# A planned attention and gated-MLP kernel: q and k of four heads transposed in one piece, and a list scheduler with other ranks and another model of TensorE

## The chip, the cores and the metric

The kernel runs on one core of a Trainium2 chip. The metric is the device time in microseconds (us) from start to end of one execution; lower is better. The engines of the core are named as in the profile: PE (TensorE, matmuls), PEld (its weight loads), DVE (VectorE), ACT (ScalarE), POOL (GpSimd) and SP (SyncE, which here only issues DMAs). Each works through its own list of instructions in order. ACT issues some DMAs as well, and such an issue stands in ACT's list.

## The reference

```python
def _attn_ref(q, k, v, g_q, g_k):            # q, k, v: [8, 12, 448, 64] float32
    q_n, k_n = (rmsnorm(q, g_q), rmsnorm(k, g_k))
    scores = (1.0 / np.sqrt(64)) * np.matmul(q_n, k_n.transpose(0, 1, 3, 2))
    scores = scores - np.max(scores, axis=-1, keepdims=True)
    attn = np.exp(scores)
    attn = attn / (np.sum(attn, axis=-1, keepdims=True) + 1e-09)
    return np.matmul(attn, v)

def _moe_ref(x, mu_k, mu_r, w_k, w_v, w_r):  # x: [8, 448, 768]; w_k [768, 1024], w_v [1024, 768], w_r [768, 768], float64
    x_prev = x shifted by one row, zeros ahead
    xk = mu_k * x + (1.0 - mu_k) * x_prev
    xr = mu_r * x + (1.0 - mu_r) * x_prev
    k = np.maximum(xk @ w_k, 0.0)
    v = k * k @ w_v
    r = 1.0 / (1.0 + np.exp(-(xr @ w_r)))
    return r * v
```

The attention's output, with its 12 heads side by side, is the `x` of the second part.

## The kernel before

**Numbers as two halves.** Each float32 matrix that PE multiplies is split into a float16 high part and a float16 low part, and a product is three products of such parts (high x high, high x low, low x high). So most data appear twice, and each split is an ACT cast (high) and a DVE or POOL subtraction (low).

**Attention, in quads and groups.** A quad is four heads (two pairs) of one batch; there are 24 quads and 48 pairs. A quad goes through these steps:

- `load`: k and q of the quad from HBM into tiles `qk` (or, early, into space lent by `xk`). The 448 rows of a head are dealt as 64 rows of 7 blocks, so that one partition holds 7 x 64 contiguous numbers, and two heads of a pair fill 64 partitions.
- `stats`: ACT squares, POOL and DVE add them up, DVE takes a reciprocal root by three Newton steps on small tiles (`sst`, `stm`, `ss`).
- `preps`: POOL multiplies by the root, ACT casts to the high part, POOL subtracts for the low part (both in a tile `nat`), and SP issues DMA transposes from `nat` to `stk`, one of 64 rows for each pair and tensor: four for a quad.
- `scores`: 168 groups, seven for a quad. A group is 128 query rows of both heads of a pair against all 448 keys (6 matmuls, two PSUM banks `sc` of five); the fourth group of a quad takes the seventh block of both pairs (12 smaller matmuls).
- `expo`, `probs`, `split`: for each of the two banks DVE takes the row maximum, ACT the exponential with its row sum, DVE turns the sum into a factor (`sums`), ACT writes the high part of the probabilities and DVE the low part (`nat`), which frees the bank. SP then transposes `nat` to `pT` (128 rows; the fourth group in two pieces of 64 rows).
- `vload`, `vprep`: v of a pair is loaded in four DMAs (`vf`), scaled and split (`vh`, `vl`).
- `attends`: 24 matmuls per pair give `ot`, which ACT copies to `x`.

**The second part, per batch.** `mix` makes `xk` and `xr` from six `x` tiles (POOL, DVE, ACT, POOL for each). `moe` then runs 144 matmuls of `xk` with `wk`, squares the result (`kf`, `kk`), and runs blocks of 18 matmuls `xr` with `wr` and 24 matmuls `kk` with `wv` for each half: three blocks for an even batch, four for an odd one. `gate` and `store` finish a block and SP stores it. There is one `xk`, one `xr` and one `kk` buffer.

**The weights** come as float64 and are turned to float32, scaled and split in 20 column tiles (`wload`, `weights`, `wsplit`): 8 of `w_k`, 6 of `w_r`, 6 of `w_v`. For tiles in `POOL_TILES` POOL scales and subtracts, for the others DVE does. The first MoE product needs the first 8 tiles and batch 0's `xk`; the first `wr` block needs all 20.

**What sets the order.** All of this is written as generators, which `Plan.run` advances as a list scheduler. Each generator offers its next instruction; the planner keeps a clock for each engine from its own price list (`price`, and the costs in `emit`), finds by `ready` when the tiles' earlier readers and writers are done, and takes the instruction with the smallest `max(clock of the engine, ready time) - 0.1 * priority`. The order in which it emits is the order in each engine's list on the chip. The priorities are the constants `PRIO_*`; `MARGIN` holds attention matmuls back until they are surely ready. In `ready`, an instruction on PE that writes the bank that the matmul before it wrote is taken to wait for that one's end and some latency.

**Rings.** Tiles come from rings with a fixed number of buffers (`QK_BUFS`, `STK_BUFS`, `NAT_BUFS` and so on).

Of the kernel before, what the change touches and what calls it, by code (L numbers as in the profile page):

```python
# [15 lines left out]
P = 128  # L16
# [12 lines left out]
QK_BUFS = 4  # L29
# [3 lines left out]
STK_BUFS = 3  # L33
# [4 lines left out]
POOL_TILES = range(2, 20, 2)  # L38
# [6 lines left out]
PRIO_P = 400  # L45
PRIO_S = 250
PRIO_A = 100
# [5 lines left out]
XK_LENT = ("nat", "nat", "qk")  # L53
PRIO_K = 100
# [3 lines left out]
PRIO_M = 400  # L58
PRIO_W = 100
W_START = 10e3  # L60
W_GAP = 9e3
W_PUSH = 0.03
F64_EXP = 2.0 ** -112
# [16 lines left out]
class Op:  # L80
    def __init__(self, eng, fn, kw, form=None):
        self.eng, self.fn, self.kw, self.form = eng, fn, kw, form
        outs = [kw[k] for k in ("out", "accum_out") if kw.get(k) is not None]
        self.reads = [span(x) for k, x in kw.items() if k not in ("out", "accum_out") and hasattr(x, "tensor")]
        self.writes = [span(x) for x in outs if hasattr(x, "tensor")]
        self.reads = [x for x in self.reads if x]
        self.writes = [x for x in self.writes if x]
# [6 lines left out]
def span(x):  # L94
    t = x.tensor
    if "DRAM" in str(t.space):
        return None
    st = x.ap[0][0]
    lo = x.offset % st if st else 0
    return t.name, lo, lo + 1 + sum(abs(s) * (n - 1) for s, n in x.ap[1:])  # L100
# [48 lines left out]
class Plan:  # L149
# [16 lines left out]
    def ready(self, ops):  # L166
        r = 0.0
        for op in ops:
            for t, lo, hi in op.reads:
                for a, b, fin, wr in self.use.get(t, ()):  # L170
                    if wr and a < hi and lo < b and fin > r:
                        r = fin
            for t, lo, hi in op.writes:
                for a, b, fin, wr in self.use.get(t, ()):
                    if a < hi and lo < b and fin > r:
                        r = fin
# [13 lines left out]
    def note(self, op, fin):  # L190
        for spans, wr in ((op.reads, False), (op.writes, True)):
            for t, lo, hi in spans:
# [4 lines left out]
                u.append((lo, hi, fin, wr))  # L197

    def emit(self, ops):
# [7 lines left out]
        if e == "PE":  # L207
            form, cost = ops[0].form
            if form != self.form:
# [6 lines left out]
        elif ops[0].fn.__name__.startswith("dma"):  # L216
# [49 lines left out]
class Ring:  # L266
# [15 lines left out]
    def get(self, early=False):  # L282
# [13 lines left out]
        if old:  # L296
            self.plan.use[name] = [(0, 1 << 30, old, True)]
        return t

    def put(self, t):  # L300
# [5 lines left out]
        self.plan.use["slot " + tag] = max(x[2] for x in self.plan.use.pop(name))  # L306
# [3 lines left out]
def rsqrt(V, y, a, t):  # L310
# [3 lines left out]
    for _ in range(NEWTON):  # L314
        yield V.tensor_tensor(out=t, in0=a, in1=y, op=ALU.mult)
        yield V.scalar_tensor_tensor(out=t, in0=t, scalar=-0.5, in1=y, op0=ALU.mult, op1=ALU.mult)
        yield V.scalar_tensor_tensor(out=y, in0=t, scalar=1.5, in1=y, op0=ALU.add, op1=ALU.mult)


def attn_moe_kernel(tc, q, k, v, g_q, g_k, mu_k, mu_r, w_k, w_v, w_r, out):  # L320
# [19 lines left out]
    mu = const.tile([P, 2, ND], F32, name="mu")  # L340
    omu = const.tile([P, 2, ND], F32, name="omu")
# [18 lines left out]
    st = {"wdone": 0, "g": 0, "moe": 0, "vl": 0, "gm": False, "mus": False, "kdone": 0}  # L360
# [11 lines left out]
    def late():  # L372
# [8 lines left out]
        "stk": Ring(ap_, [P, 2, 2 * NT, HD], F16, "stk", STK_BUFS, plan),  # L381
        "pT": Ring(ap_, [P, 2 * NT, S], F16, "pT", PT_BUFS, plan),
# [11 lines left out]
    }  # L394
    HOME = {}
# [44 lines left out]
    def mu_stats():  # L440
        yield A.dma_start(out=mu[:, 0, :], in_=mu_k.rearrange("(t p) -> p t", p=P))
        yield A.dma_start(out=mu[:, 1, :], in_=mu_r.rearrange("(t p) -> p t", p=P))
        yield V.tensor_scalar(out=omu, in0=mu, scalar1=-1.0, scalar2=1.0, op0=ALU.mult, op1=ALU.add)
# [3 lines left out]
        yield V.tensor_scalar(out=u, in0=mu, scalar1=2.0, scalar2=-1.0, op0=ALU.mult, op1=ALU.add)  # L447
# [13 lines left out]
    def load():  # L461
        for u in range(NQ):
            b, j = quads[u]
            ts = []
            for n, src in enumerate((k, q)):
                t = yield from R["qk"].get(u < 3)
                for x in range(2):
                    h0 = 4 * j + 2 * x
                    yield (A if u < 2 else SP).dma_start(out=t[x * HD:(x + 1) * HD], in_=src[b, h0:h0 + 2].rearrange("h (r t) d -> r h (t d)", t=NT))
                ts.append(t)  # L470
            LD[u] = ts

    def stats():
        for u in range(NQ):
            yield from until(lambda: u in LD and st["gm"])
# [3 lines left out]
            for n, t in enumerate(LD[u]):  # L479
# [7 lines left out]
                if n == 0:  # L487
                    yield G_.tensor_tensor(out=tv, in0=tv, in1=bcast(G[:, :], 2 * NT), op=ALU.mult)
            yield V.tensor_scalar(out=ss[:, 0:2 * NT], in0=ss[:, 0:2 * NT], scalar1=1.0 / HD, scalar2=1e-6, op0=ALU.mult, op1=ALU.add)
            yield V.tensor_scalar(out=ss[:, 2 * NT:NSS], in0=ss[:, 2 * NT:NSS], scalar1=gm[:, 3:4], scalar2=gm[:, 4:5], op0=ALU.mult, op1=ALU.add)  # L490
            yield from rsqrt(V, y, ss, tm)
            SS[u] = y

    def preps():
        for u in range(NQ):
            yield from until(lambda: u in SS)
            y = SS.pop(u)
            X = []
            for x in range(2):
                t = yield from R["stk"].get(u < 3)  # L500
                X.append(t)
            for n, t in enumerate(LD.pop(u)):
                tv = t.rearrange("p h (t d) -> p (h t) d", d=HD)
                yield G_.tensor_tensor(out=tv, in0=tv, in1=spread(y[:, 2 * NT * n:2 * NT * (n + 1)], HD), op=ALU.mult)
                nat = yield from R["nat"].get(u < 3)
                hi, lo = heads(nat, 0), heads(nat, NT * P)
                t4 = t.rearrange("p h (t d) -> p h t d", d=HD)
                yield A.copy(out=hi, in_=t4)
                yield G_.tensor_tensor(out=lo, in0=t4, in1=hi, op=ALU.subtract)
                R["qk"].put(t)  # L510
                for x in range(2):
                    yield SP.dma_start_transpose(out=X[x][:, n], in_=nat[x * HD:(x + 1) * HD].rearrange("p a c -> p (a c)"))
                R["nat"].put(nat)
            for x in range(2):
                TQ[2 * u + x] = X[x]
# [45 lines left out]
    def batch_scales(b):  # L561
# [14 lines left out]
    def scores():  # L576
        for gi, (u, x, t0) in enumerate(groups):
            yield from until(lambda: 2 * u + x in TQ and len(banks["sc"].free) > 1)
# [6 lines left out]
            for m, (kl, ql) in enumerate(((0, 0), (0, 1), (1, 0))):  # L585
                for i in (2 * u + 1, 2 * u) if both_pairs else (2 * u + x,):
                    X = TQ[i]
                    for h in (1, 0):
# [10 lines left out]
            if t0 == NT - 1:  # L599
                R["stk"].put(TQ.pop(2 * u))  # L600
            elif x and t0 == NT - 3:
                R["stk"].put(TQ.pop(2 * u + 1))
            sums = ring_sum[gi % 6]
            D = {}
            for j in range(2):
                plan.spawn(expo(gi, j, both[j], sums, D), PRIO_E)
            plan.spawn(probs(gi, both, sums, D), PRIO_E)

    def expo(gi, j, sp, sums, D):
        yield V.tensor_reduce(out=sums[:, j:j + 1], in_=sp[:, 0:S], axis=AX.X, op=ALU.max, negate=True)  # L610
        yield A.activation(out=sp[:, 0:S], in_=sp[:, 0:S], func=AF.Exp, bias=sums[:, j:j + 1], accum_out=sp[:, S:S + 1])
        D[j] = True

    def probs(gi, both, sums, D):
        u, x, t0 = groups[gi]
        yield from until(lambda: len(D) == 2 and st["g"] == gi)
        for i in (2 * u, 2 * u + 1) if t0 == NT - 1 else (2 * u + x,):
            if i not in PT:
                PT[i] = yield from R["pT"].get()
# [5 lines left out]
        for j, sp in enumerate(both):  # L625
            yield V.tensor_scalar(out=r[:, j:j + 1], in0=sp[:, S:S + 1], scalar1=1e-9, scalar2=2.0 ** -15, op0=ALU.add, op1=ALU.mult)
# [6 lines left out]
        if t0 < NT - 1:  # L633
            yield SP.dma_start_transpose(out=PT[2 * u + x][:, :, t0 * HD:(t0 + 2) * HD], in_=phf)
            CNT[2 * u + x] += 1
        else:
            for y in range(2):
                yield SP.dma_start_transpose(out=PT[2 * u + y][:, :, t0 * HD:], in_=phf[y * HD:(y + 1) * HD])
                CNT[2 * u + y] += 1
# [286 lines left out]
```

## Time and profile before

| | before |
|---|---|
| median of 3 runs | 1139.08 us (1138.01 to 1139.62) |
| the profiled execution | 1136.72 us |
| its span, first to last instruction | 1134.6 us |
| mean granted TensorE clock | 0.952 |
| busy: PE, DVE, ACT, POOL | 917.6, 846.7, 757.7, 664.2 us |
| DMA packets, data moved | 480,163, 161.76 MB |
| first score matmul, first MoE matmul | 56.6, 197.7 us |
| last attend matmul ends | about 1003.4 us |

A row of the profile names the line of the kernel, the engine, the operation and the tiles (output, arrow, inputs). Every instruction is recorded at one line of the planner's `emit`, so the rows are told apart by their tiles. In a row of a group, `| busy, mean ns of one | idle time of the engine just before them` follow the count. DMA issues and semaphore waits are not counted as busy, so SP has no share of its own; its queue is read from rows with `SPq`, which give the shortest, median and longest duration of an issue. Matmuls are pipelined, so busy time of PE is more than the time that its columns need.

### The profile page before, as it was taken

The numbers are of one execution on the slowest core, as the hardware profiler recorded it, in microseconds if no ns is written. First come the engines' busy times: TensorE is split into PE (matmuls) and PEld (weight loads), VectorE is DVE, ScalarE is ACT, GpSimd is POOL, SyncE is SP. The second block draws the span as 40 slices with busy tenths as digits, with TensorE's granted clock in tenths as the row PEclk, the third lists the DMA queues.
The fourth block names the chain that finished last, engine by engine and source line by source line (L and its number), as shares of the span: only waits on it lengthen the run. The fifth ranks groups of instructions, "written<-read, shape, count | busy, mean of one in ns | idle before, by whom it ended". The sixth has DMA issues, their size and how long they took to land. (4 is left out here: it accounts for less than half of the span.)

```text
span 1134.6 us, 18939 instructions
## 1 busy us (share of the span) xinstructions
PE 917.6 (81%) x6031; PEld 474.5 (42%) x6031; DVE 846.7 (75%) x2254; ACT 757.7 (67%) x1750; POOL 664.2 (59%) x668
## 2 busy tenths in 40 slices
PE   1346445968989889898889898989898899999997
PEld 0112222424444444444444454444444444455564
DVE  5898797997899589879888987889786879822000
ACT  3577475896779577777778776788577768832310
POOL 2733328785678465685668574877486636463611
PEclk9996665989999999999999999999999999999999
DMA  9999999876988888897998888889886989811011
GB/s 194 196 182 181 168 188 208 156 142 129 170 168 143 160 146 165 154 156 146 147 167 150 155 161 158 156 141 171 148 141 125 171 135 159 140 26 28 14 29 28
DMA packets 480163, 161.76 MB, mean 143 GB/s; under 512 B 447296, under 2 KB 476480, under 8 KB 480064
## 3 DMA queue, kind: packets, MB, share of 16 engines
q1 hardware_dynamic: 459808, 141.42, 71.1%
q10 hardware_dynamic: 20256, 19.15, 6.8%
q8 instruction: 47, 0.77, 0.3%
q14 instruction: 52, 0.43, 0.1%
HBM read 50.40 MB, written 11.01 MB: 54 GB/s over the span
## 5 line engine op out<-in xcount | busy, mean ns | idle before, releaser
L205 ACT ACTIVATE sc<-sc,sums 128x448 f32<-128x448 f32 x336 | 201.1, 620 | 70.9 <-DVE sums L205 68.0
L205 PE MATMUL mm<-wvh,kk 128*128 128x384 f16 x896 | 236.3, 328 | 5.6 <-DVE o L205 4.7
L205 DVE SCALAR_TENSOR_TENSOR nat<-sc,sums,nat 128x448 f16<-128x448 f32 x316 | 201.2, 673 | 27.1 <-ACT nat L205 26.5
L205 PE MATMUL mm<-xk,wkh 128*128 128x448 f16 x768 | 209.9, 355 | 6.5 <-ACT kf L205 4.2
L205 DVE TENSOR_REDUCE sums<-sc 128x1 f32<-128x448 f32 x336 | 194.0, 611 | 18.5 <-PE sc L205 18.4
L205 ACT ACTIVATE nat<-sc,sums 128x448 f16<-128x448 f32 x316 | 187.7, 662 | 24.6 <-DVE sums L205 7.3
L205 PE MATMUL sc<-stk 64*128 64x448 f16 (+1 forms) x1152 | 133.8, 382 | 78.0 <-DVE nat L205 52.3
L205 PE MATMUL mm<-wrh,xr 128*128 128x384 f16 x672 | 177.3, 328 | 0.0
L205 PEld LDWEIGHTS <-kk 128*128 128x128 f16 (+1 forms) x1362 | 129.6, 99 | 110.9 <-issue 28.5
L205 PE MATMUL ot<-pT,vh 128*64 128x448 f16 x768 | 123.2, 376 | 39.6 <-DMA pT<-nat 20.2
L205 PE MATMUL mm<-wvl,kk 128*128 128x384 f16 x448 | 147.0, 328 | 0.0
L205 PE MATMUL mm<-xk,wkl 128*128 128x448 f16 x384 | 136.0, 354 | 0.0
L205 PEld LDWEIGHTS <-xr 128*128 128x128 f16 x1008 | 96.3, 98 | 73.8 <-issue 12.0
L205 POOL TENSOR_TENSOR nat<-qk,nat 128x896 f16<-128x896 f32 x45 | 87.7, 1948 | 65.9 <-ACT nat L205 65.7
L205 DVE SCALAR_TENSOR_TENSOR df<-x,bsc,df 128x448 f32<-128x448 f32 x96 | 99.8, 1050 | 29.2 <-POOL df L205 28.8
L205 POOL TENSOR_TENSOR o<-o,bsc 128x384 f32<-128x384 f32 x48 | 43.7, 910 | 117.2 <-DVE o L205 83.2
L205 PE MATMUL mm<-wrl,xr 128*128 128x384 f16 x336 | 109.9, 327 | 0.0
L205 PEld LDWEIGHTS <-stk 64*128 64x128 f16 (+1 forms) x1152 | 45.6, 101 | 150.4 <-issue 100.1
L205 PEld LDWEIGHTS <-wkh 128*128 128x128 f16 x768 | 70.8, 98 | 88.7 <-issue 31.9
L205 DVE SCALAR_TENSOR_TENSOR o<-o,mm 128x384 f32<-128x384 f32 x56 | 30.5, 544 | 94.6 <-PE mm L205 67.3
L205 POOL TENSOR_TENSOR kf<-kf 128x448 f32<-128x448 f32 x64 | 62.6, 979 | 56.1 <-ACT kk L205 54.1
L205 ACT ACTIVATE o<-mm,bsc 128x128 f32<-128x128 f32 x144 | 43.3, 386 | 70.1 <-PE mm L205 52.0
(129 smaller groups left out, 1625.0 us busy)
## 6 DMA issues: line engine op xcount, KB each, us to landing
out_dram<-o SPq DMA_DIRECT2D x56, 192.0 KB, 3.1
qk<-in_k_dram SPq DMA_DIRECT2D x44, 224.0 KB, 3.8
qk<-in_q_dram SPq DMA_DIRECT2D x42, 224.0 KB, 3.8
vf<-in_v_dram SPq DMA_DIRECT2D x96, 64.0 KB, 3.1
raw<-in_moe_w_v_dram ACTq DMA_DIRECT2D x12, 512.0 KB, 5.0
vf<-in_v_dram SPq DMA_DIRECT2D x96, 48.0 KB, 2.8
raw<-in_moe_w_r_dram ACTq DMA_DIRECT2D x12, 384.0 KB, 5.8
kk<-in_moe_w_k_dram ACTq DMA_DIRECT2D x8, 384.0 KB, 6.9
```

Source lines behind the costliest of these rows:

```text
L205: r = op.fn(op.kw["out"], op.kw["value"]) if op.fn.__name__ == "memset" else op.fn(**op.kw)
```

## The change

In the kernel's work:

- `stk` holds a quad instead of a pair: one transpose of 128 rows each for k and q. Two such tiles instead of three of half the size; three `qk` tiles instead of four.
- So that the blocks of q come out side by side, q is loaded in eight DMAs per quad (runs of 64 numbers) instead of two (runs of 448).
- `pT` of both pairs of a quad is one tile of two halves, and the seventh block's probabilities go there in one transpose of 128 rows. The odd pair's blocks stand in another order, and its copy from `ot` to `x` is done in two parts.
- The two row sums of a group are written side by side in the first bank, and one DVE instruction works on both. The scales of `mix` and of the output are made in fewer instructions.
- Quad 0's multiplies and subtractions go to DVE (`Q_DVE`), 13 weight tiles instead of 9 to POOL, and the weight loads wait until the first group is past its exponential (`W_G0`). The first pieces of k and q are loaded ahead of v and the weights.

In the scheduler: `span` tells the two halves of partitions and of `pT` apart; `ready` no longer lets a PE instruction wait for an earlier one on PE; priorities are other numbers, and some rise while `moe` waits for something (`st["want"]`, `BOOST_*`) or while few groups are left before a quad's data are needed (`near`, `SLACK_*`). `NEWTON_ON` stays on DVE and the three `*_SLOW` factors are 1.

The diff, cut to what the steps of the prediction touch:

```diff
-QK_BUFS = 4
+QK_BUFS = 3
-STK_BUFS = 3
+STK_BUFS = 2
-POOL_TILES = range(2, 20, 2)
+POOL_TILES = range(1, 14)
-PRIO_P = 400
+PRIO_P = 200
-PRIO_A = 100
+PRIO_A = 50
-XK_LENT = ("nat", "nat", "qk")
-PRIO_K = 100
+XK_LENT = ("qk", "qk", "nat")
+PRIO_K = 0
+BOOST_K = 500
+BOOST_R = 500
+BOOST_A = 300
+BOOST_W = 300
+BOOST_Q = 400
+SLACK_S = 3
+SLACK_Q = 2
+W_G0 = 1
+LOAD_A = 2
+Q_DVE = 1
...
                 for a, b, fin, wr, pe in self.use.get(t, ()):
-                    if wr and a < hi and lo < b and fin > r:
+                    if wr and not (pe and op.eng == "PE") and a < hi and lo < b and fin > r:
...
+                        for t0 in range(x, NT - 1, 2):
+                            o = t0 // 2 * 4 * HD
+                            yield D(out=tf[x * HD:(x + 1) * HD, o:o + 4 * HD].rearrange("p (h d) -> p h d", d=HD),
+                                    in_=src[b, 4 * j:4 * j + 4].rearrange("h (r t) d -> r h t d", t=NT)[:, :, t0, :])
...
-                for x in range(2):
-                    yield SP.dma_start_transpose(out=X[x][:, n], in_=nat[x * HD:(x + 1) * HD].rearrange("p a c -> p (a c)"))
+                yield SP.dma_start_transpose(out=X[:, n], in_=nat.rearrange("p a c -> p (a c)"))
...
-                            lhsT=X[hs, 1, ql * NT + t0:ql * NT + t0 + n].rearrange("p t c -> p (t c)"),
-                            rhs=X[hs, 0, kl * NT:(kl + 1) * NT].rearrange("p t c -> p (t c)"),
+                            lhsT=X[hs, 1, ql * NT + t0, o:o + HD] if both_pairs else X[hs, 1, ql * NT + t0 + i % 2, :],
+                            rhs=X[hs, 0, kl * NT:(kl + 1) * NT, o:o + HD],
...
-        for j, sp in enumerate(both):
-            yield V.tensor_scalar(out=r[:, j:j + 1], in0=sp[:, S:S + 1], scalar1=1e-9, scalar2=2.0 ** -15, op0=ALU.add, op1=ALU.mult)
+        yield V.tensor_scalar(out=r, in0=both[0][:, S:S + 2], scalar1=1e-9, scalar2=2.0 ** -15, op0=ALU.add, op1=ALU.mult)
...
-            for y in range(2):
-                yield SP.dma_start_transpose(out=PT[2 * u + y][:, :, t0 * HD:], in_=phf[y * HD:(y + 1) * HD])
+            yield SP.dma_start_transpose(out=PTQ[:, :, S - HD:S + HD], in_=phf)
...
+                yield from until(lambda: st["g"] >= W_G0 + W_G1 * ci)
                 raw = yield from R["raw"].get(ci < NF)
```

Three places show how the instructions stand. First PE around its first score matmul, before (`kk` is lent space for a weight tile, `dg` and `ones` belong to that tile's scale):

```order
L205 LDWEIGHTS kk0_102
L205 MATMUL ot0_462<-kk0_102 128x128
L205 MATMUL ot0_462<-dg_473,ones_87 128x128
L205 LDWEIGHTS stk0_281
L205 MATMUL sc1_458<-stk0_281 128x448
```

and now, from the start of PE's list (`vs` belongs to v's scale):

```order
L227 MATMUL ot0_157<-ident_70,mucol_144 2x128
L227 MATMUL ot0_157<-ident_70,allmax_165 128x2
L227 LDWEIGHTS vs_171
L227 MATMUL ot0_188<-ident16_75,vs_171 128x128
L227 LDWEIGHTS vs_206
L227 MATMUL ot0_219<-ident16_75,vs_206 128x128
L227 LDWEIGHTS stk0_228
L227 MATMUL sc1_258<-stk0_228 128x448
```

The scores of quad 0 now come ahead of all weight tiles; before, six tiles came first.

Second, SP's list around the first transposes, before:

```order
L205 DMA vf0_94<-in_v_dram 64x4x64
L205 DMA vf1_95<-in_v_dram 64x4x64
L205 DMA xk0_103<-in_q_dram 64x2x448
L205 DMA_TRANSPOSE stk0_281<-nat1_284 128x14x64
L205 DMA vf1_95<-in_v_dram 64x3x64
L205 DMA xk0_103<-in_q_dram 64x2x448
```

and now (`x3` is three in a row):

```order
L227 DMA_TRANSPOSE stk0_228<-nat1_232 128x14x128
L227 DMA vf1_94<-in_v_dram 64x3x64
L227 DMA_TRANSPOSE stk0_228<-nat3_250 128x14x128
L227 DMA vf1_94<-in_v_dram 64x4x64
L227 DMA qk2_243<-in_k_dram 64x2x448 x2
L227 DMA xk0_103<-in_q_dram 64x4x64 x3
L227 DMA xk0_103<-in_q_dram 64x2x64
```

One transpose serves both pairs, and a quad's q stands there as two such runs of four issues.

Third, PE behind its last attend matmul, before:

```order
L205 MATMUL ot0_11694<-pT1_11465,vh1_11500 64x448
L205 LDWEIGHTS xr0_11096
L205 MATMUL mm1_11752<-wrh_90,xr0_11096 128x384
L205 LDWEIGHTS xr0_11096
L205 MATMUL mm1_11752<-wrl_91,xr0_11096 128x384
```

and now:

```order
L227 MATMUL ot0_11693<-pT_101,vh1_11463 64x448
L227 LDWEIGHTS kk0_10815
L227 MATMUL mm1_11734<-wvh_91,kk0_10815 128x384
L227 LDWEIGHTS kk0_10815
L227 MATMUL mm1_11734<-wvl_92,kk0_10815 128x384
```

Before, all three blocks of batch 6 and all of batch 7 come after it, 732 matmuls; now batch 6 is in the second half of its blocks, and 588 matmuls are left.

More of the change, by code (lines that the diff above doesn't have):

```diff
@@ L58 @@
 PRIO_M = 400
+BOOST_K = 500
[5 more added lines that the diff above has]
+SLACK_Q = 2
+BOOST_V = 0
+SLACK_V = 2
 PRIO_W = 100
 W_START = 10e3
-W_GAP = 9e3
+W_G0 = 1
+W_G1 = 0
+LOAD_A = 2
+PRIO_L = 0
+Q_DVE = 1
+W_GAP = 10e3
 W_PUSH = 0.03
+NEWTON_ON = "DVE"
+OP_SLOW = 1.0
+DMA_SLOW = 1.0
+PE_SLOW = 1.0
 F64_EXP = 2.0 ** -112
@@ L96, in span @@
     if "DRAM" in str(t.space):
[L97 to L100, printed above, removed]
+        return []
+    st, n = x.ap[0]
+    p, lo = divmod(x.offset, st) if st else (0, 0)
+    hi = lo + 1 + sum(abs(s) * (c - 1) for s, c in x.ap[1:])
+    if t.name.startswith("pT"):
+        lo %= 2 * S
+        hi = lo + x.ap[-1][1]
+    return [((t.name, e), lo, hi) for e in range(2) if p < HD * (e + 1) and p + n > HD * e]
 def width(x):
@@ L208, in emit @@
             form, cost = ops[0].form
+            cost *= PE_SLOW
             if form != self.form:
@@ L296, in get @@
         if old:
-            self.plan.use[name] = [(0, 1 << 30, old, True)]
+            self.plan.use[name, 0], self.plan.use[name, 1] = [(0, 1 << 30, old, True, False)], [(0, 1 << 30, old, True, False)]
         return t
@@ L305, in put, with rsqrt @@
             return
-        self.plan.use["slot " + tag] = max(x[2] for x in self.plan.use.pop(name))
+        self.plan.use["slot " + tag] = max(x[2] for e in range(2) for x in self.plan.use.pop((name, e), [(0, 0, 0.0, True, False)]))
         self.free.append(tag)
-def rsqrt(V, y, a, t):
+def rsqrt(V, y, a, t, pool=None):
     ti = t.bitcast(I32)
@@ L577, in scores @@
         for gi, (u, x, t0) in enumerate(groups):
-            yield from until(lambda: 2 * u + x in TQ and len(banks["sc"].free) > 1)
+            yield from until(lambda: u in TQ and len(banks["sc"].free) > 1)
             both = []
@@ L783, in wsplit @@
             st["rsc"] = True
+        if st["wdone"] == NW:
+            yield V.tensor_scalar(out=WIN[:, NF:NF + ND], in0=WIN[:, NF:NF + ND], scalar1=smu[:, 1:2], scalar2=0.5, op0=ALU.mult, op1=ALU.mult)
+            yield V.tensor_scalar(out=WIN[:, NF + ND:NW], in0=WIN[:, NF + ND:NW], scalar1=wsc[:, 1:2], scalar2=0.5, op0=ALU.mult, op1=ALU.mult)
+            yield V.tensor_scalar(out=WIN[:, NF + ND:NW], in0=WIN[:, NF + ND:NW], scalar1=wsc[:, 1:2], scalar2=None, op0=ALU.mult)
+            st["wout"] = True
     def prod(ps_, la, ra, n, w):
@@ L816, in moe @@
             off = (b % 2) * HD
-            yield from until(lambda: XKN.get(b) == ND and st.get("rsc") and st["wdone"] >= NA)
+            st["want"] = "xk"
+            yield from until(lambda: XKN.get(b) == ND)
+            st["want"] = "w"
+            yield from until(lambda: st.get("rsc") and st["wdone"] >= NA)
+            st["want"] = None
             xk, sc = XK[b], BSC[b]
```

151 lines of the change are left out of this document (86 added, 65 removed).

## The prediction

> **What bounds the kernel now.** I read the page's engine shares and slices first, then a table of stages, then who waits for whom in the long stage, then the start, the SP queue and the end.
>
> ```profile
> PE 917.6 (81%) x6031; PEld 474.5 (42%) x6031; DVE 846.7 (75%) x2254; ACT 757.7 (67%) x1750; POOL 664.2 (59%) x668
> ```
>
> No engine is full on average, so the stages decide. I cut the span at the first scores (57 us), the first MoE matmul (198), and the last attend (1003.4):
>
> ```profile
> 0.00:57.00 57.00, 14.40 (x65) 7.92 (x67) 39.43 (x135) 23.98 (x38) 26.60 (x28) 1.00 0.95 195
> 57.00:198.00 141.00, 69.21 (x404) 31.93 (x401) 117.91 (x345) 92.58 (x202) 61.44 (x55) 0.71 0.95 186
> 198.00:965.00 767.00, 673.60 (x4582) 345.99 (x4580) 644.23 (x1672) 582.68 (x1373) 508.98 (x507) 0.98 0.86 153
> 1003.40:1134.60 131.20, 123.64 (x734) 71.46 (x732) 19.84 (x32) 29.13 (x71) 49.34 (x56) 0.99 0.09 22
> ```
>
> Columns after the length are busy us of PE, PEld, DVE, ACT and POOL, then granted clock, DMA share, GB/s. Until 198 us PE mostly waits for data (114.4 us idle); DVE is the fullest compute engine, 118 of 141 us. From 198 to 965 us PE is idle 767.0-673.6 = 93.4 us and DVE is at 84%: two in-order queues that feed each other. After 1003.4 us only MoE matmuls are left. Who ends PE's and DVE's idle time in the long stage:
>
> ```profile
> PE sc L205 <- DVE nat L205: 36.3, 37, 6.4
> PE ot L205 <- DMA pT<-nat: 15.9, 14, 2.1
> PE sc L205 <- DMA stk<-nat: 10.3, 6, 2.4
> PE ot L205 <- ACT x L205: 8.0, 12, 2.2
> DVE sums L205 <- ACT sc L205: 26.3, 38, 2.6
> DVE nat L205 <- ACT nat L205: 25.2, 42, 2.1
> ```
>
> PE's largest wait is for a score bank that DVE's last softmax step (nat) frees. The softmax chain DVE, ACT, DVE, ACT, DVE paces the stage, and MoE matmuls queued behind a waiting score matmul wait with it.
>
> **The change part by part.**
>
> *1. Less work on DVE.*
>
> ```profile
> L205 DVE TENSOR_SCALAR sums<-sc 128x1 f32<-128x1 f32 x336 | 46.7, 147 | 30.4 <-ACT sc L205 29.0
> L205 DVE TENSOR_SCALAR bsc<-WIN,bsc 128x6 f32<-128x6 f32 x16 | 9.5, 595 | 0.3
> L205 DVE TENSOR_SCALAR bsc<-mu,bsc 128x6 f32<-128x6 f32 x16 | 4.2, 261 | 0.1
> L205 DVE TENSOR_SCALAR bsc<-omu,bsc 128x6 f32<-128x6 f32 x16 | 3.6, 223 | 0.0
> L205 DVE SCALAR_TENSOR_TENSOR bsc<-bsc 128x1 f32<-128x1 f32 x8 | 4.1, 512 | 0.1
> L205 DVE TENSOR_TENSOR bsc<-bsc,smu 128x1 f32<-128x1 f32 x8 | 3.6, 454 | 0.0
> L205 DVE TENSOR_TENSOR bsc<-bsc,wsc 128x1 f32<-128x1 f32 x8 | 2.4, 302 | 0.0
> L205 DVE SCALAR_TENSOR_TENSOR wrl<-wf,WSC,wrh 128x768 f16<-128x768 f32 x3 | 4.0, 1337 | 0.1
> L205 DVE SCALAR_TENSOR_TENSOR vl<-vf,bstat,vh 128x512 f16<-128x512 f32 x48 | 53.3, 1111 | 9.8 <-ACT vh L205 8.9 <-DMA stk<-nat 0.4 <-DMA qk<-in_q_dram 0.4
> ```
>
> Both row sums of a group now lie side by side in one bank and one instruction turns them: 336 become 168, so 168 x 147 ns = 24.7 us less. The mix scales lose 16 instructions of about 0.24 us (3.9 us), the output scales the three bsc rows of 128x1 (4.1+3.6+2.4 = 10.1 us), with three of 595 ns added once (1.8 us). POOL_TILES from 9 to 13 weight tiles takes four splits of about 1.34 us from DVE (5.3 us) and gives each to POOL. Quad 0's five multiplies and subtractions come to DVE; it shows no such 128x896 form, so I bound one between 1.1 us (the 128x512 row) and 2.2 us (twice it) and take the lower end, 5.5 us, since this runs once and before other work. Sum: about -37 us of 846.7, of which some 32 lie after 198 us. That the chain loses one 147 ns step per group is in this sum.
>
> *2. Transposes of 128 rows, and q in pieces, on SP.* SP is not counted as busy, but its queue is long:
>
> ```profile
> L205 SPq DMA_TRANSPOSE pT<-nat x180: 1230/1736/5242, 64.0 to 995.4; - x180
> L205 SPq DMA_TRANSPOSE stk<-nat x94: 1245/1328/3477, 36.7 to 951.8; - x94
> L205 SPq DMA_DIRECT2D qk<-in_q_dram x42: 595/740/1333, 67.0 to 890.5; - x42
> SPq L205 <- DVE nat L205: 87.3, 42, 4.4
> SPq L205 <- DVE sums L205: 62.7, 48, 4.0
> ```
>
> Per quad two pairs of stk transposes and one pair for the seventh block become three whole ones: 6 x 1.33 us against 3 x 1.74 us, 2.8 us saved. q comes in 8 issues instead of 2: 6 x 0.60 to 6 x 0.74 us, 3.6 to 4.4 us added. Over 24 quads that is +19 to +38 us on SP. SP still waits 87.3 and 62.7 us for DVE in the long stage, so I put it at nothing; if that cover goes, the eight issues (4.8 to 5.9 us on end) stand ahead of a due pT transpose, and PE's attend matmuls wait for it. Whole transposes land as pT's do, 0.4 us later than stk's (rows below); the second stk quad covers that.
>
> ```profile
> qk<-in_q_dram SPq DMA_DIRECT2D x42, 224.0 KB, 3.8
> vf<-in_v_dram SPq DMA_DIRECT2D x96, 64.0 KB, 3.1
> pT<-nat SPq DMA_TRANSPOSE x180, 4.4
> stk<-nat SPq DMA_TRANSPOSE x94, 4.0
> q1 hardware_dynamic: 459808, 141.42, 71.1%
> ```
>
> In packets: q's runs fall from 1792 to 256 bytes, 43,008 packets for 6,144. At q1's mean (0.711 x 1134.6 x 16 / 459,808 = 28 ns) the 36,864 more take 65 us of the 16 engines, which lifts the long stage's share from 0.86 to about 0.92: hidden as long as it stays below one. The vf rows, already in 256-byte runs, land in 3.1 us. The Trainium skill (DMA: Bandwidth & Descriptors, "Why small descriptors are slow (HBM only)") speaks against this edit: a 256-byte descriptor pays 27% overhead, and its Specifications ask for 512 bytes for line rate. By it, as an estimate, q's 11 MB would cost a quarter more DMA time, less than the bound above, and the sum would be the same.
>
> *3. The start.* Now quad 0's k and q stand ahead of weights and v, its multiplies leave POOL, and weight loads wait for the first softmax.
>
> ```profile
> 17.08 0.93 ACT L205 ACTIVATE xk<-xk 128x896 f32<-128x896 f32 x1
> 22.31 0.93 ACT L205 ACTIVATE xk<-qk 128x896 f32<-128x896 f32 x1
> 28.13 1.69 POOL L205 TENSOR_TENSOR xk<-xk,ss 128x896 f32<-128x896 f32 x1 [3.69 <-DVE ss L205]
> 50.27 1.89 POOL L205 TENSOR_TENSOR xk<-qk,xk 128x896 f16<-128x896 f32 x1 [1.05 <-ACT xk L205]
> 56.59 2.42 PE L205 MATMUL sc<-stk 64*128 64x448 f16 x12 [1.52 <-DMA stk<-xk]
> ```
>
> k's square starts at 17.1 us, q's at 22.3, q's last subtraction only at 50.3, the scores at 56.6. With q in by about 11 us (eight issues of 0.6 us on each of two queues, 3.8 us to land, and 2 us of slack), 6 us from square to root (22.3 to 28.1), 7 us of prep (four DVE steps of 1.1 us, two ACT casts near 0.93 us, a wait) and 6 us of transpose (1.74 us of issue, 4.4 to land), plus a V split of 1.1 us twice between, scores should start near 32 us. But that is 25 us earlier on PE only: the first MoE matmul now stands after 29 score steps of six matmuls, not 26, and the weight work that filled DVE before 57 us comes after. DVE's work up to that point is 157 us before; I count about 155 after. With 14 us of it done by 33 us and the rest at the old 84%, the first MoE matmul falls at 33+168 = 201 us; at 90% it falls at 190. I take 195, -3 us.
>
> *4. The order.* PE has 6,010 matmuls in both orders, but 732 stand behind the last attend before and 588 now: 144 MoE matmuls move into the attention stage.
>
> ```profile
> 1077.00 45.02 PE mm L205 x276
> ```
>
> At 45.02/276 = 163 ns the dense end shortens by 23.5 us. That is a gain only where the 144 fill PE's idle time; otherwise the last attend moves later by as much. So I don't add it, I use it to size what the 93.4 us of idle give back. Nothing to lose: all 93.4. Nothing won: 0. DVE's 32 us less, three quarters of it on the chain that PE waits for, give 24; the moved matmuls, half of them in idle time, 11. Together -35 us.
>
> *5. Small edits.*
>
> ```profile
> L205 ACT ACTIVATE o<-mm,bsc 128x128 f32<-128x128 f32 x144 | 43.3, 386 | 70.1 <-PE mm L205 52.0 <-issue 18.0
> L205 PE MATMUL sc<-stk 64*128 64x448 f16 x864 | 114.1, 380 | 73.8 <-DVE nat L205 48.2 <-DMA stk<-nat 15.1 <-DVE xk L205 7.1
> L205 PE MATMUL mm<-xk,wkh 128*128 128x448 f16 x768 | 209.9, 355 | 6.5 <-ACT kf L205 4.2 <-ACT xk L205 0.8 <-POOL xk L205 0.8
> L205 ACT ACTIVATE nat<-qk 128x896 f32<-128x896 f32 x45 | 43.2, 960 | 29.0 <-DMA qk<-in_q_dram 13.2 <-DMA pT<-nat 11.4 <-issue 4.4
> ```
>
> The odd pairs' output copy in two parts adds 24 ACT instructions, at most 0.39 us each by the row of the 128x128 gate, 9 us on an engine at 76% in the long stage: hidden. Score matmuls read k in seven runs of 64 columns; no row shows that, and I take the present 380 ns; the other form of that width has 355, so 25 ns either way on 576 pairs, 14 us. Three qk tiles for four: a load may start later. ACT's squares wait 13.2 us for q now; doubled it would cost as much again, on ACT, which has room. Nothing taken.
>
> **Sum:** 1134.6 - 3 - 35 = 1096.6 us of span. The profiled execution took 1136.7, 2.1 over its span, and the median 1139.1 is 2.4 above that: about 1100.
>
> **Rivals.**
> *PE becomes the bound.* If the new order lets PE run nearly dense, idle falls from 93.4 to about 30 us and the start gives 10: 1139-63-10 = 1066. For it: waits for DVE are 36.3 us, and DVE gets 5% lighter. Against: the waits for DMA, ACT and banks come from other places.
> *The gain stays off the path.* ACT's steps of the chain are not shorter (DVE waits 26.3 and 25.2 us for it), so the 37 us turn into DVE idle time and the tail's 23.5 us move ahead of the last attend: 1122 to 1141.
> *Slower: SP's bursts.* Eight q issues instead of two hold SP 3.6 to 4.4 us longer, in each of 24 quads, with a pT transpose behind them: up to 106 us. If 3 us of each reach PE's attends, that is +72 against -38: 1173. It decides from 38/24 = 1.6 us per quad on. For it: SP issues all the time already, and waits for pT are PE's second largest (15.9 us). Against: SP's 150 us of waiting for DVE, and a gap in its queue that the q loads can take.
>
> **How the numbers follow.** Forecast (1075 to 1122) 0.55; dense PE 0.14; off the path 0.20, a quarter of it within 0.2% (about what a measurement of this kernel can tell); SP's bursts 0.11. Faster 0.84, same 0.05, slower 0.11. The range 1064 to 1142 leaves out the slower case and the far half of dense PE.
>
> **What would show it.** Right: first scores near 32 us, first MoE matmul near 195; DVE near 810 us; PE's wait for DVE nat well under 36 us; last attend near 990 and about 108 us behind it. Wrong: waits of PE for pT or stk that grow, SP waiting for DVE much less, or a first MoE matmul after 205 us.

## The result, and the profile after

| | before | after |
|---|---|---|
| median (lowest to highest) | 1138.55 us (1136.40 to 1139.62, 4 runs) | 1107.88 us (1102.53 to 1109.23, 4 runs) |
| ratio, 95% interval | | 0.9724 [0.9688, 0.9761] |
| profiled execution, its span | 1136.72, 1134.6 us | 1106.79, 1105.0 us |
| first score matmul | 56.6 us | 31.9 us |
| first MoE matmul | 197.7 us | 202.3 us |
| last attend ends, PE work behind it | 1003.4, 131.2 us | 999.8, 105.2 us |

The kernel is 31 us faster: the forecast was 1100 us in 1064 to 1142. By stages the span's 29.6 us are +4.6 us up to the first MoE matmul, -8.2 us from there to the last attend (805.7 to 797.5 us), and -26.0 us behind it.

The shares of the engines, and `q1`, the DMA queue that SP's transfers go through, from the page of the kernel after:

```profile
PE 919.8 (83%) x6031; PEld 470.0 (43%) x6031; DVE 811.5 (73%) x2050; ACT 773.5 (70%) x1774; POOL 668.6 (61%) x671
q1 hardware_dynamic: 494512, 141.88, 69.5%
```

DVE lost 35.2 us, ACT gained 15.8. The queue moved 34,704 packets more in a smaller share of a shorter span.

The table of stages of the kernel after, cut at its own first scores (32 us), the old ones (57), its first MoE matmul (202), 965 us and its last attend. Columns as in the prediction's table: length, busy time of PE, PEld, DVE, ACT and POOL, granted clock, DMA share, GB/s:

```profile
0.00:32.00 32.00, 1.66 (x7) 0.92 (x9) 15.74 (x59) 9.93 (x14) 8.64 (x15) 1.00 0.63 118
32.00:57.00 25.00, 11.57 (x62) 5.22 (x58) 20.12 (x64) 13.53 (x29) 5.72 (x5) 1.00 0.79 218
57.00:202.00 145.00, 70.21 (x405) 33.29 (x404) 117.39 (x333) 96.66 (x208) 73.22 (x67) 0.71 0.95 191
202.00:965.00 763.00, 702.84 (x4730) 354.93 (x4731) 619.34 (x1515) 604.89 (x1404) 529.57 (x524) 0.97 0.83 155
999.80:1105.00 105.20, 99.29 (x587) 57.14 (x585) 14.04 (x21) 22.69 (x54) 37.74 (x42) 1.00 0.09 23
```

In the long stage PE is idle 763.0 - 702.8 = 60.2 us, where it was 93.4; 4730 matmuls fit into 763 us, where 4582 took 767. Behind the last attend stand 587 matmuls for 734. Who ends the idle time between 202 and 965 us (PE, DVE, then SP's queue; total, times, longest):

```profile
PE sc L227 <- DVE nat L227: 16.5, 18, 6.2
PE mm L227 <- ACT kf L227: 12.0, 11, 7.0
PE sc L227 <- DMA stk<-nat: 7.1, 5, 3.8
PE ot L227 <- DMA pT<-nat: 1.4, 2, 1.2
...
DVE nat L227 <- ACT nat L227: 34.4, 53, 2.0
DVE sums L227 <- ACT sc L227: 24.2, 45, 1.8
...
SPq L227 <- DVE sums L227: 100.2, 54, 7.7
SPq L227 <- DVE nat L227: 70.8, 30, 6.4
```

PE's waits for a score bank (16.5 us, 36.3 before) and for `pT` (1.4, 15.9 before) are most of what went; its wait for ACT at `kf` grew (12.0, 4.7 before). DVE still waits for ACT in the softmax chain, 58.6 us for 51.5 before. SP waits for DVE 171 us, more than the 150 before. By these lines SP looks idle enough; the experiments show that this reading is wrong.

SP's issues in the kernel after: shortest, median and longest duration in ns, first and last start in us.

```profile
L227 SPq DMA_DIRECT2D qk<-in_q_dram x168: 604/615/1534, 83.9 to 919.1; - x168
L227 SPq DMA_TRANSPOSE pT<-nat x164: 1329/2048/5624, 53.2 to 991.6; - x164
L227 SPq DMA_TRANSPOSE stk<-nat x47: 1309/1647/5535, 24.6 to 957.1; - x47
```

### The profile page after: what moved, and what is told of

Same layout as the page of the kernel before. It is cut to its first block, busy times and chain, and to the rows that moved or that the text cites. A ratio compares the mean times of both kernels' runs of the same rounds, so it can differ in the third digit from the quotient of the medians.

```text
span 1105.0 us, 18967 instructions
## 1 busy us (share of the span) xinstructions
PE 919.8 (83%) x6031; PEld 470.0 (43%) x6031; DVE 811.5 (73%) x2050; ACT 773.5 (70%) x1774; POOL 668.6 (61%) x671
## 3 DMA queue, kind: packets, MB, share of 16 engines
q1 hardware_dynamic: 494512, 141.88, 69.5%
## 5 line engine op out<-in xcount | busy, mean ns | idle before, releaser
L227 ACT ACTIVATE sc<-sc,sums 128x448 f32<-128x448 f32 x336 | 204.1, 610 | 73.5 <-DVE sums L227 64.2
L227 DVE SCALAR_TENSOR_TENSOR nat<-sc,sums,nat 128x448 f16<-128x448 f32 x328 | 213.7, 676 | 41.7 <-ACT nat L227 38.8
L227 PE MATMUL mm<-wvh,kk 128*128 128x384 f16 x896 | 233.8, 326 | 3.4 <-ACT kf L227 2.2
L227 ACT ACTIVATE nat<-sc,sums 128x448 f16<-128x448 f32 x328 | 193.0, 644 | 19.4 <-DMA pT<-nat 6.2
L227 PE MATMUL sc<-stk 64*128 64x448 f16 (+1 forms) x1152 | 136.9, 389 | 64.5 <-DVE nat L227 39.5
L227 PE MATMUL mm<-wrh,xr 128*128 128x384 f16 x672 | 180.3, 332 | 3.1 <-POOL xr L227 2.6
L227 DVE SCALAR_TENSOR_TENSOR df<-x,bsc,df 128x448 f32<-128x448 f32 x96 | 106.7, 1124 | 14.1 <-POOL df L227 13.9
L227 POOL TENSOR_TENSOR qk<-qk,ss 128x896 f32<-128x896 f32 x45 | 79.9, 1775 | 54.2 <-DVE ss L227 35.6
L227 POOL TENSOR_TENSOR nat<-qk,nat 128x896 f16<-128x896 f32 x44 | 85.1, 1934 | 34.7 <-ACT nat L227 32.6
L227 DVE SCALAR_TENSOR_TENSOR o<-o,mm 128x384 f32<-128x384 f32 x56 | 30.6, 546 | 85.7 <-PE mm L227 58.6
```

The costliest lines, as they stand in the source:

```text
L227: r = op.fn(op.kw["out"], op.kw["value"]) if op.fn.__name__ == "memset" else op.fn(**op.kw)
```

## The experiments

Each kernel was timed in five rounds beside the kernel before on its chip. To set the kernels beside each other, an effect against the kernel after is (its ratio - 0.9724) x 1138.6 us; the intervals of two ratios make it uncertain by 4 to 6 us. "PE idle" is, in each trace, the length from the first MoE matmul to the end of the last attend less PE's busy time in it, from a table of stages cut there; it is 95.0 us before and 60.5 after. "SP issue time" is the sum of the durations of all DMA issues in SP's queue: 780.6 us before, 796.6 after. The stretch of the kernel before:

```profile
197.70:1003.40 805.70, 710.66 (x4839) 363.35 (x4838) 669.82 (x1746) 612.33 (x1440) 526.79 (x531) 0.99 0.86 151
```

| kernel | median us | ratio, 95% interval | against after, us | PE idle us | matmuls behind the last attend | SP issue time us |
|---|---|---|---|---|---|---|
| after | 1107.9 | 0.9724 [0.9688, 0.9761] | | 60.5 | 587 | 797 |
| `e2_two_sums` | 1106.2 | 0.9725 [0.970, 0.975] | 0 | 60.9 | 587 | 792 |
| `e12_dve_more` | 1119.4 | 0.9844 [0.9814, 0.9874] | +14 | 71.0 | 587 | 789 |
| `e3_half_transposes` | 1297.3 | 1.1389 [1.1366, 1.1412] | +190 | 198.4 | 587 | 1062 |
| `e3b_merged_undone` | 1169.7 | 1.029 [1.026, 1.032] | +64 | 101.3 | 587 | 882 |
| `e10_q_two_loads` | 1088.8 | 0.9576 [0.9547, 0.9604] | -17 | 49.2 | 587 | 697 |
| `e3c_halves_planned` | 1207.9 | 1.0619 [1.0595, 1.0643] | +102 | 122.2 | 479 | 865 |
| `e17_stores_act` | 1166.8 | 1.0277 [1.0238, 1.0316] | +63 | 103.3 | 479 | 755 |
| `e1_pe_model_undone` | 1143.8 | 1.0047 [1.0032, 1.0063] | +37 | 85.1 | 713 | 783 |
| `e7_no_boost` | 1159.0 | 1.0193 [1.017, 1.0217] | +53 | 81.7 | 515 | 771 |
| `e6_start_undone` | 1114.4 | 0.9806 [0.9779, 0.9832] | +9 | 72.9 | 551 | 779 |
| `e4_other_margin` | 1109.2 | 0.9763 [0.9728, 0.9798] | +4 | 62.7 | 581 | 796 |
| `e5_before_pe_model` (before, one edit) | 1127.5 | 0.9896 [0.9877, 0.9915] | -12 against before | 80.5 | 497 | 772 |

The first five experiments keep the order of the kernel after: the planner plans as it did, and only where an instruction is handed to the chip is it split, doubled, replaced or left out. The others plan anew, and each list changes in many places.

**The row sums (same order).** The one DVE instruction on both sums becomes two again.

```diff
+    def parts(self, op):
+        if op.kw.get("scalar1") == 1e-9:
+            return [dict(op.kw, out=op.kw["out"][:, j:j + 1], in0=op.kw["in0"][:, j:j + 1]) for j in range(2)]
+        return [op.kw]
...
-                r = op.fn(op.kw["out"], op.kw["value"]) if op.fn.__name__ == "memset" else op.fn(**op.kw)
...
+            for kw in self.parts(op):
...
+                    r = op.fn(kw["out"], kw["value"]) if op.fn.__name__ == "memset" else op.fn(**kw)
...
```

> The changed kernel in the same order on every engine, but the factor of each group's two row sums is again made by two DVE instructions (168 more of about 147 ns, 24.7 us on DVE), which the planner doesn't know of. Theory 1 (DVE's softmax chain and the new order each carry part of the gain): 10 to 18 us of it come back, 1118 to 1126 us. Theory 2 (the new order alone carries it, a few per cent more or less on DVE don't matter): within 3 us of the changed kernel's 1108. Theory 3 (the whole transposes carry it by freeing SP and the DMA engines): 1108 as well.

No loss: 0.9725 against 0.9724. The rows by shape, of after and of this kernel:

```profile
L227 DVE TENSOR_SCALAR sums<-sc 128x2 f32<-128x2 f32 x168 | 25.5, 152 | 27.4 <-ACT sc L227 26.7
```

```profile
L233 DVE TENSOR_SCALAR sums<-sc 128x1 f32<-128x1 f32 x336 | 36.3, 149 | 25.8 <-ACT sc L233 25.0
```

168 more instructions of 149 ns cost 10.8 us of busy time, not 25.0, since two that follow each other overlap, and nothing of the kernel's time that stands out of the uncertainty. That is half of what the change took from this row, 46.7 - 25.5 = 21.2 us (forecast: 24.7, the largest single part of the DVE term): in the trace before, only 64 of the 168 pairs stood side by side. No run puts back the whole of it.

**More DVE work on the chain (same order).** A row maximum is taken twice where the planner's count of steps is divisible by six: 53 more of 0.616 us, 32.6 us on DVE. It tests the credit given to 32 us of DVE.

```diff
+        if op.kw.get("negate") and self.n % 6 == 0:
+            return [op.kw, op.kw]
...
```

> The changed kernel in the same order, but 53 of the 336 row maxima of the scores are taken twice, which the planner doesn't know of: 53 x 0.614 us = 32.5 us more for DVE, on the softmax chain. It puts back by time what the change took from DVE (35.2 us). Theory 1 (the prediction: three quarters of DVE's time on the chain is the kernel's time): 24 us more, 1128 to 1136. Theory 2 (the order carries the gain, and DVE has room in it): less than 10 us more, 1108 to 1117.

+14 us by the ratios, +6.7 us by the profiled spans (1111.7 against 1105.0). The median, 1119.4 us, lies between the two expected ranges. Its stretch from the first MoE matmul to the last attend, of after and of this kernel:

```profile
202.30:999.80 797.50, 737.04 (x4976) 373.38 (x4976) 643.91 (x1575) 630.44 (x1471) 542.95 (x544) 0.97 0.82 153
```

```profile
202.30:1006.20 803.90, 732.87 (x4974) 372.54 (x4974) 670.36 (x1622) 630.49 (x1469) 541.00 (x544) 0.98 0.80 152
```

Of 32.6 us between a fifth and two fifths reach the end, not three quarters; the rest goes into waits of DVE. This is work added to a finished order; that work taken away counts by the same fraction is not shown.

**All transposes in halves (same order).** Each of the 216 transposes of 128 rows is issued as two of 64.

```diff
+        if op.fn.__name__ == "dma_start_transpose":
+            return [dict(op.kw, out=op.kw["out"][:, :, x * HD:(x + 1) * HD], in_=op.kw["in_"][x * HD:(x + 1) * HD]) for x in range(2)]
...
```

> The changed kernel in the same order, but every transpose (of q, k and probabilities, 216 of 128 rows) is issued as two of 64 rows, 432 in all, which the planner doesn't know of. By the rows of before a half takes 1.33 us on SP and a whole one 1.74 to 2.05, so SP issues some 130 to 200 us more, with the bytes unchanged. Theory 1 (SP and DMA have room): up to 10 us more, 1108 to 1118. Theory 2 (the order): the same. Theory 3 (SP and DMA freed by whole transposes carry the gain): 1125 us or more, at or above the kernel before.

+190 us, far outside what hidden issues allow. The issues of this kernel:

```profile
L233 SPq DMA_TRANSPOSE pT<-nat x328: 1230/1732/2832, 54.9 to 1184.3; - x164
...
L233 SPq DMA_TRANSPOSE stk<-nat x94: 1229/1708/2747, 24.8 to 1144.3; - x94
```

A half takes nearly as long to issue as a whole (medians 1732 for 2048, 1708 for 1647 ns). SP then issues for 1062 us of a span of 1296.5. This splits transposes that were whole before too, so it shows that issues on SP are not hidden, and gives no price of the change.

**Only the merged transposes in halves (same order).** The same, for the `stk` transposes and the seventh block's `pT`: 72 more issues, so 288 transposes, as before.

```diff
+        if op.fn.__name__ == "dma_start_transpose" and (op.kw["out"].tensor.name.startswith("stk") or op.half):
...
```

> The changed kernel in the same order; only the transposes that the change merged (48 of k and q, 24 of the seventh blocks) are issued as halves again, 72 more issues, which the planner doesn't know of. With all 216 halved SP issued DMAs for 1062 of 1190 us up to the last attend and the kernel took 190 us more. Theory 1 (SP has room up to about 85% of its time, and is the bound above that): SP goes from 797 to about 870 us of issues, 87% of 1000 us, and 10 to 35 us are lost: 1118 to 1143. Theory 2 (the cost is one for each issue, 190/216 = 0.88 us): 63 us, 1171. Theory 3 (the prediction: SP's waits for DVE hide it): within 5 us of 1108.

+64 us, 0.9 us for each issue, as theory 2 had it. Its stretch, and what PE, ACT, DVE and SP wait for between 202 and 1000 us:

```profile
204.20:1062.90 858.70, 757.38 (x4974) 378.84 (x4974) 642.44 (x1575) 632.00 (x1470) 539.55 (x544) 0.94 0.78 143
...
PE sc L233 <- DMA stk<-nat: 35.2, 13, 4.5
...
ACT nat L233 <- DMA stk<-nat: 40.3, 17, 5.4
ACT nat L233 <- DMA qk<-in_q_dram: 27.8, 5, 6.7
ACT nat L233 <- DMA pT<-nat: 24.6, 23, 3.8
...
DVE nat L233 <- ACT nat L233: 51.7, 59, 4.8
DVE sums L233 <- PE sc L233: 40.3, 25, 4.4
...
SPq L233 <- DVE sums L233: 113.0, 62, 6.8
SPq L233 <- DVE nat L233: 53.8, 27, 5.7
```

The same rows of the kernel after in that window:

```profile
PE sc L227 <- DMA stk<-nat: 7.1, 5, 3.8
...
ACT nat L227 <- DMA pT<-nat: 12.7, 12, 3.4
ACT nat L227 <- DMA stk<-nat: 7.4, 5, 3.3
ACT nat L227 <- DMA qk<-in_q_dram: 6.8, 3, 2.9
...
DVE nat L227 <- ACT nat L227: 35.6, 55, 2.0
DVE sums L227 <- PE sc L227: 21.6, 18, 4.0
...
SPq L227 <- DVE sums L227: 103.2, 55, 7.7
SPq L227 <- DVE nat L227: 71.0, 31, 6.4
```

These rows show that SP's waits for DVE are no cover: SP has 85 us more to issue, and its waits for DVE are 166.8 us where they were 174.2 (189.7 over the whole of its longer stretch), so the added issues did not come out of them. What grew is PE's wait for `stk` (35.2 for 7.1 us) and ACT's waits (92.7 for 26.9): a transpose that is issued late keeps its `nat` buffer, of which there are four, and ACT waits to write the next probabilities or the next q and k there. DVE then waits longer for ACT and for scores (92.0 for 57.2 us). It would close the circle if SP's waits for DVE came from SP's own lateness, round through ACT and DVE, but that is not shown: with 100 us less to issue, in the next experiment, they are longer (191.1 us), not shorter. The DMA engines are not fuller (share 0.78 for 0.82). Whether SP's lateness in general costs the time, or only that the second half of a tile lands one issue later, is not told apart.

**q in two loads (same order).** From quad 1 on, q is loaded by two DMAs a quad in runs of 448 numbers, as before, in place of eight. Its blocks then lie in other places than the scores read them from, so its output is not the reference's; the work on PE, DVE, ACT and POOL is the same.

```diff
+                        if u:
+                            whole = D(out=t[x * HD:(x + 1) * HD], in_=src[b, h0:h0 + 2].rearrange("h (r t) d -> r h (t d)", t=NT))
...
```

> The changed kernel in the same order, but from the second quad on q is loaded in two DMAs per quad with runs of 448 numbers, as before, at the places of the fourth and the eighth; the six others are left out. q's blocks then lie in the wrong places of the tile, so the output is not the reference's; every other instruction stays. SP issues 138 DMAs less, some 85 us, and the DMA engines get 35,000 packets less. Theory 1 (SP near its bound): 10 to 30 us less, 1078 to 1098. Theory 3 (SP's waits hide the eight issues): within 5 us of 1108.

-17 us, for 100 us less of SP issue time. The DMA queue, the stretch, the loads' issues, and SP's waits for DVE between 202 and 1000 us:

```profile
q1 hardware_dynamic: 458608, 141.87, 69.5%
...
198.50:982.60 784.10, 734.90 (x4974) 372.29 (x4974) 647.14 (x1575) 629.15 (x1470) 541.60 (x544) 0.98 0.82 156
...
L235 SPq DMA_DIRECT2D qk<-in_q_dram x42: 597/1089/1334, 82.5 to 901.8; - x42
...
SPq L235 <- DVE sums L235: 100.6, 53, 7.6
SPq L235 <- DVE nat L235: 90.5, 45, 7.4
```

So q in pieces costs the kernel after some 17 us. Whether the 132 issues or the 35,904 packets that SP has less gave the time is not told apart here. The Trainium skill (DMA: Bandwidth & Descriptors, "Why small descriptors are slow (HBM only)") gives a 256-byte descriptor 27% overhead. No run here shows it: the packets of `q1` took 0.695 x 1087.9 x 16 = 12,097 us of engine time in this kernel and 0.695 x 1105.0 x 16 = 12,288 in the kernel after, but the kernel with more DVE work, with all of the packets, had 0.681 x 1111.7 x 16 = 12,113.

**The halves with a planner that knows of them.** Here the planner itself plans halves, at the prices it had before.

```diff
-                w, iss, tot = n / 128 * 1.21, 1510, 4000
+                w, iss, tot = n / 128 * 1.21, 1510 if n > 2e5 else 1240, 4000 if n > 2e5 else 3500
...
-                yield SP.dma_start_transpose(out=X[:, n], in_=nat.rearrange("p a c -> p (a c)"))
+                for x in range(2):
+                    yield SP.dma_start_transpose(out=X[:, n, :, x * HD:(x + 1) * HD], in_=nat[x * HD:(x + 1) * HD].rearrange("p a c -> p (a c)"))
...
```

> The changed kernel planned again with the merged transposes as halves (72 more issues), so that the planner knows of them and prices a half as before. With the same order and unknown to the planner they cost 62 us. Theory 1 (SP's issues are near the bound, whatever the plan knows): 25 us or more are still lost, 1130 to 1165. Theory 2 (most of the 62 us came from a plan that was surprised by them): 1108 to 1122.

+102 us, more than with the order left alone, and above both expected ranges. Between 202 and 1000 us ACT waits longest for transposes again:

```profile
ACT nat L227 <- DMA pT<-nat: 59.8, 35, 4.3
```

The planner's knowledge of the halves doesn't win the loss back. How much of the 102 us is another order and how much the halves is not told apart.

**Stores issued by ACT.** The 56 stores go from SP's queue to ACT's, planned anew.

```diff
-                yield SP.dma_start(out=r[tt], in_=o[e * HD:(e + 1) * HD, :])
+                yield A.dma_start(out=r[tt], in_=o[e * HD:(e + 1) * HD, :])
```

> The changed kernel planned again with the 56 output stores issued by ACT instead of SP: SP issues some 38 us less, ACT the same more. Theory 1 (SP's queue is nearer the bound than ACT): by the 0.14 us for each issue that the q loads gave, about 8 us less, 1097 to 1104. Theory 2 (ACT, at 79% in the long stage, pays as much): 1106 to 1120.

+63 us: neither theory gave that. SP's issue time fell to 755 us and the kernel still became slower, so SP's sum alone does not set the time of another order. PE waits 28.3 us for ACT between 202 and 1000 us, where it waits 12.0 after:

```profile
PE mm L227 <- ACT kf L227: 28.3, 19, 7.5
```

A store in ACT's list can make ACT wait for the store's data, with `kf` behind it; that this is the cause, rather than the other order, was not shown.

**The model of TensorE.** Undone in the kernel after, and then made alone in the kernel before.

```diff
...
-                    if not (pe and op.eng == "PE") and a < hi and lo < b and fin > r:
+                    if a < hi and lo < b and fin > r:
```

The line for reads is changed back in the same way.

> The changed kernel, planned again with the old model of TensorE: an instruction on PE waits in the plan for the end of an earlier one on the same bank. Behind the last attend 714 matmuls are left instead of 588 (732 before). Theory 1: about half of the gain goes, since the moved matmuls come back behind the attention: 1117 to 1125 us. Theory 2: nearly all of it goes, 1130 or more. Theory 3: 1108.

> The kernel before, planned again with the new model of TensorE alone (an instruction on PE doesn't wait in the plan for an earlier one on PE); same instructions, 498 matmuls left behind the last attend instead of 732. Theory 1: about half of the gain, 1120 to 1130 us. Theory 2: most of it, 1105 to 1117. Theory 3: none, 1136 to 1140.

Undoing it costs 37 us: the whole gain and, within the uncertainty, no less. Making it alone in the kernel before gives 12. The stretches of the two:

```profile
202.90:1016.80 813.90, 728.77 (x4848) 365.25 (x4848) 627.20 (x1569) 627.75 (x1457) 528.39 (x533) 0.96 0.79 150
```

```profile
198.20:1031.70 833.50, 752.98 (x5072) 387.87 (x5071) 681.24 (x1753) 621.88 (x1463) 539.69 (x546) 0.97 0.82 147
```

Without it, PE idles 85.1 us instead of 60.5 and the last attend ends at 1016.8 us. In the kernel before, 234 matmuls (732 to 498 in the plan) move ahead of the last attend, worth 234 x 163 ns = 38 us at the end, but that attend moves from 1003.4 to 1031.7 us and gives 28 back.

**The boosts.** All five `BOOST_*` are zero.

> The changed kernel planned again with all five priority boosts at 0, so that no generator is raised for what the second part waits for. The first MoE matmul then stands after 37 score steps instead of 29. Theory 1 (the mended model of TensorE carries the order's part of the gain, the boosts a little): 1110 to 1125. Theory 2 (the boosts carry it): 1130 or more.

+53 us. The stretch begins at the first MoE matmul, 31 us later than in the kernel after:

```profile
233.50:1061.50 828.00, 746.26 (x4984) 382.90 (x4982) 647.98 (x1521) 610.88 (x1417) 522.00 (x535) 0.97 0.76 144
```

Fewer matmuls stand behind its last attend (515) than in the kernel after, and it is slower: the count alone says nothing.

**The start.** `W_G0` and `Q_DVE` zero, the first loads on their old queues and with their old priority.

> The changed kernel planned again with the start of before: weight loads from the first moment, quad 0's multiplies and subtractions on POOL, the first k and q of two quads on ACT's queue. Theory 1 (the start only shifts work; the first MoE matmul fell at 202 us after and 198 before): within 8 us of 1108 either way. Theory 2 (first scores 25 us earlier are worth something): 1118 or more.

+9 us, not twice the uncertainty, although its first MoE matmul comes 8 us earlier, at 194.1:

```profile
194.10:1011.60 817.50, 744.57 (x5022) 380.06 (x5022) 637.68 (x1583) 631.67 (x1474) 542.27 (x545) 0.97 0.80 151
```

PE idles 12 us more behind it. A first MoE matmul that comes early is no gain by itself.

**Another plan of the same kind.** `MARGIN` 780 for 800, a change of the order with no meaning of its own, to see how much one plan differs from the next.

> The changed kernel planned with MARGIN 780 instead of 800, a change with no meaning of its own: it shows how far the time moves when the planner merely comes to another order (582 matmuls behind the last attend instead of 588). If orders of one planner lie close together: within 5 us of 1108. If the order is a matter of luck: 10 us or more either way, and the differences between the replanned kernels are to be read with that width.

+4 us, within the uncertainty. So of the replanned kernels, differences of some 5 us can be noise of planning; 37, 53, 63 and 102 are far above that, and the 9 us of the start are not. One other plan is one sample: it doesn't say how far plans can lie apart.

## Why the prediction was right, and where it was not

**The whole.** Time, sign and the mechanism of term 4 came out: PE idle in the long stage 60.2 us for a forecast 93.4 - 35 = 58, the dense end 26.0 us shorter for 23.5, DVE at 811.5 us for 810, first scores at 31.9 us for 32. The last attend ended at 999.8 us for 990, with 105.2 us behind it for 108. Of the 8.4 us by which the span missed 1096.6, 7.6 are the start's. But the right total was made of terms that were wrong in both directions, and that they came to the right sum is luck.

**Term 1, DVE.** The busy time was right to 2 us. The step that failed is "three quarters of it on the chain that PE waits for", 24 us. Row sums doubled (10.8 us of busy time) cost nothing, and 32.6 us more on the chain cost 7 to 14. If work taken away counts by the same fraction, DVE's 32 us less are worth 7 to 13 us. "DVE is at 84%" was read as DVE pacing the stage: the rows in which DVE itself waits for ACT, 26.3 and 25.2 us, spoke against it and were put with the rival.

**Term 2, SP.** The issue times were about right (+16 us in the trace for +19 to +38). What failed is "SP still waits 87.3 and 62.7 us for DVE in the long stage, so I put it at nothing". Neither part is nothing: merging the transposes is worth 64 us in the order of the kernel after, and loading q in pieces costs 17 of them. The difference, some 47 us in the change's favour if the two add (no run undoes both), was left out of the sum. The DMA share went the other way as well: 0.83 for a forecast 0.92. The step that failed there is one price for every packet: q1's mean was 28 ns before and 0.695 x 1105.0 x 16 / 494,512 = 25 ns after.

**Term 3, the start.** -3 us was +4.6: the first MoE matmul came at 202.3 us, a microsecond outside the bounds of 190 to 201, and 7 after the value taken. DVE's work up to it was right, 153 us for 155. The 90% that DVE was given is the step: it was busy 117.4 of 145 us, 81%, between 57 and 202 us. What a start is worth is another thing than when that matmul comes: undone, it came 8 us earlier, and the kernel was no faster (+9 us). (In the trace of the kernel before, seven weight tiles stand ahead of the first scores, not six.)

**Term 4, the order.** The step "the moved matmuls, half of them in idle time, 11" holds the only price put on the scheduler, and it was too low: its parts are worth 37 us (the model of TensorE) and 53 us (the boosts), each with all else in place. They don't add: the first alone in the kernel before gives 12. The forecast's 35 us of idle were right as a sum, with DVE's part too large, by the experiments, and the order's and SP's too small.

**Small edits.** The copies from `ot` to `x` took 37.7 us on ACT for 31.4, 6 us more for a forecast 9; whether they are covered was not tested. ACT's waits for q in the long stage fell from 13.2 to 6.8 us, so three `qk` tiles did no harm there. The score matmuls that read k in seven runs took 388 ns on the mean for 380, inside the 25 ns allowed.

**The rivals.** SP's bursts are real, and their price was too high: 17 us over 24 quads is 0.7 us for each, below the 1.6 us from which that rival decides, and its condition did not show (PE's waits for `pT` fell to 1.4 us). For DVE's part, "the gain stays off the path" was the better account; its time was not, since the idle time of PE was filled by other parts of the change. A dense PE would have needed 30 us of idle; q in two loads comes nearest, with 49.2.

## What to carry to other kernels

An engine that issues DMAs has no busy share on the page, so add up its issues; and don't take its waits for room: here 85 us more of issues cost 64 us, and the waits stayed as long as they were. Test a credit such as "three quarters of this engine's saving" by adding the same work once in an unchanged order: one run gives a fraction, though for work added and not for work taken away. Parts of a planned order don't add up, and neither a count of moved matmuls nor an early start of the next stage is a gain until PE's idle time says so.

## What the runs showed of the hardware

- **Transposes on SP.** A DMA transpose of 64 rows takes nearly as long to issue as one of 128 (shortest 1.23 against 1.31 to 1.33 us; medians 1.73 against 2.05 us for `pT`, 1.71 against 1.65 for `stk`). In the same order, 697, 797, 882 and 1062 us of SP issue time went with 1089, 1108, 1170 and 1297 us: 0.2 us of time for each us of issues up to 797, and about 0.7 beyond. The first step is q's loads and the others are transposes, so the two slopes can come from the kind as well as from the amount.
- **The clock where PE waits.** With the same matmuls in the same order, the granted clock in the stretch was 0.98 at 49 us of idle, 0.97 at 60, 0.94 at 101 and, all transposes halved, 0.92 at 198; from 60 us of idle on, PE's busy time for them rose from 737.0 to 757.4 and to 781.8 us. The last of these:

```profile
210.70:1190.90 980.20, 781.80 (x4974) 392.62 (x4974) 632.01 (x1575) 634.72 (x1469) 538.26 (x544) 0.92 0.71 125
```

So of the 61 us by which the merged transposes' undoing lengthened the stretch, 41 are waiting and 20 slower matmuls. Why the clock falls is not shown by these runs; the 71 us of idle with more DVE work went with 0.98.
- **Short DVE instructions.** Two that follow each other, each listed at 149 ns, add 64 ns of busy time for the second (10.8 us over 168).
